# Batch 0's k and q loaded in layouts that TensorE turns, its first products in two halves, the residual summed apart, and a new order of the work

## The chip, the cores and the metric

The kernel runs on one core of a Trainium2 chip. The core has five engines that work side by side, each through its own list of instructions in order: TensorE (PE, the matrix products; PEld is its weight load), VectorE (DVE), ScalarE (ACT), GpSimd (POOL) and SyncE (SP), which issues the transfers from and to the chip's memory. The metric is the device time in microseconds (us); lower is better.

## The reference

Eight batches of 576 rows. For each batch there is first an attention without scores: q gets a softmax over the 64 channels of a head, k a softmax over the 576 rows, and the product of k and v (64x64 a head) is applied to q. The result x (576x512) goes through a gated feed-forward layer whose gate mixes rows.

```python
q_s = softmax(q, axis=-1)                  # over the 64 channels of a head
k_s = softmax(k, axis=2)                   # over the 576 rows
x = q_s @ (k_s.T @ v)                      # per head, 8 heads of 64 -> 576 x 512
u, v = gelu(x @ w_in) halves               # 512 each
v_n = (v - mean) / sqrt(var + 1e-6) * g_ln # over the 512 channels
v_s = w_sg @ v_n + b_sg                    # mixes the 576 rows
out = x + (u * v_s) @ w_out
```

## The kernel before

Everything is float32. The three large products (x with w_in, v_n with w_sg, the gated values with w_out) are made of three TensorE products each: both sides are split into a high part and a low part in a rounded type, and high by high, high by low and low by high are summed in one PSUM bank. The names end in `_h` and `_l` for these parts.

The work is cut into steps named after what they do, with the batch as first number, and one written list, `PLAN`, gives the order of all 1248 steps. The loop over `PLAN` calls the steps one after the other; the wrapper `InOrder` chains each engine's instructions, so every engine does its own part of the list in that order, and an engine whose next instruction waits holds back all that stands behind it. SP's transfers follow the list too. All of the recording goes through a few helper lines, so nearly all rows of the trace have one of two line numbers (L153 for the helper, L241 for TensorE).

The steps that matter here, for batch b and half h (four heads):
- Start: `load_w_in f` brings one of eight column blocks of w_in, 512 KB, as pairs of words; `wi_a` (ACT), `wi_b`, `wi_c`, `wi_d` (DVE) put float32 words together, `wi_h` (ACT) rounds the high part, and the low part is `wi_l`: either on another engine, or `wi_x` (TensorE: the word minus its high part, into PSUM) and a copy by ACT. Blocks 0 to 3 serve `hu`, blocks 4 to 7 `hv`. `w_sg` (`ws_`) and `w_out` (`wo_`) go the same way.
- k: `load_k`, the maximum over rows `k_ma`, `k_mb`, `k_mc` (DVE), then across partitions: for batches 0 and 1 by TensorE (`kt_mm`, `k_top`, `kb_mm`), for the others on DVE and ACT; `k_sub`, `k_exp`, the product with v `kv_mm`, `kv_inv`, `kv_scale`.
- q lies in 32-row blocks with half a head's channels in a row: `q_max`, `q_swapm`, `q_top`, `q_sub`, `q_exp`, `q_sum`, `q_swapd`, `q_inv`, `q_mul`, and `q_turn`, DVE's transpose in 32x32 blocks, which gives `qt` with channels on partitions.
- `x_mm` makes x, `x_high` and `x_low` split it (for batch 0 some low parts through `x_neg` on TensorE).
- `hu_mm` and `hv_mm` are x with w_in (four and, with the shared tail, four and a half a batch), `hu_gelu`, `hv_gelu` their activations, `hv_stat`, `hv_pow`, `hv_norm`, `hv_high`, `hv_low` the normalization and its split; `sg_mm` mixes rows, `gate`, `gate_high`, `gate_low` make the gated values, `out_mm` the last product, `out_add` adds x's high part out of PSUM, `out_rest` its low part, `out_store` stores. The very last block goes in two halves (`last_mm`, `last_add`, `last_rest`, `last_store`).

PSUM has three double banks (`ps2`, for x, hu, sg and out) and two single ones (`ps1`, for hv, kv and the small products), taken in turn; a product that takes a bank waits until the bank's reader is done. `kk`, `vv` and `qq` have two buffers each, one for each half.

## Time and profile before

| what | value |
|---|---|
| median of three runs | 515.95 us (515.62 to 517.37) |
| span of the profiled execution | 515.4 us |
| PE busy | 484.6 us (94%) |
| DVE busy | 365.9 us (71%) |
| ACT busy | 272.9 us (53%) |
| POOL busy | 125.3 us (24%) |

The span reaches from the first to the last instruction of the profiled execution; no other time of that execution is recorded, so what lies around the span is taken as the 0.55 us by which the median of the runs exceeds it. A busy share is an average over the whole span: in this kernel the stages have different limits, so the stretches are read one by one.

### The profile page before, as it was taken

How to read it: one execution, taken by the hardware profiler on the slowest of the kernel's cores; microseconds unless marked ns; L12 is line 12 of the kernel's file. 1: busy time of each engine (PE TensorE's matmuls, PEld its weight loads, DVE VectorE, ACT ScalarE, POOL GpSimd, SP SyncE). 2: the span in 40 equal slices, each digit the busy share in tenths (PEclk: the TensorE clock that was granted, in tenths of full speed). 3: DMA queues.
4: the chain of work that ended last, by engine and by line, in shares of the span. 5: the costliest groups of instructions: out<-in, count | busy, mean ns of one | idle time of the engine just before them, and what ended most of it. 6: DMA issues, size and time to landing. Idle time of an engine off the chain costs nothing.

```text
span 515.4 us, 9389 instructions
## 1 busy us (share of the span) xinstructions
PE 484.6 (94%) x3809; PEld 441.9 (86%) x3809; DVE 365.9 (71%) x640; ACT 272.9 (53%) x600; POOL 125.3 (24%) x106
## 2 busy tenths in 40 slices
PE   0678998999999999999999999999999999999996
PEld 0347876998999789998999889999989889999996
DVE  6999999999898998487956888658734662145222
ACT  4885977765763574755474356752439054323110
POOL 0333454333140430322023210112200311123312
PEclk9888999999999999999999999999999999999999
DMA  8977160031513402040421441033200020000103
GB/s 304 384 265 285 51 243 5 16 134 39 181 48 126 156 36 93 1 178 1 142 75 48 153 171 30 17 93 155 76 1 1 1 93 1 0 1 25 46 1 116
DMA packets 19055, 48.87 MB, mean 95 GB/s; under 512 B 1602, under 2 KB 8132, under 8 KB 19012
## 3 DMA queue, kind: packets, MB, share of 16 engines
q1 hardware_dynamic: 19012, 48.28, 26.5%
q8 instruction: 30, 0.49, 0.4%
q14 instruction: 13, 0.11, 0.1%
HBM read 38.83 MB, written 9.44 MB: 94 GB/s over the span
## 4 chain that ended last, share of the span: by engine, by line
PE 80%; DVE 12%; DMA 3%; issue 2%; ACT 1%; SPq 1%; POOL 0%; DVEq 0%; ACTq 0%
PE ps L241 80%; DVE km L153 2%; DMA kk<-k 2%; DVE ot_i L153 2%; DMA raw_vnh<-w_in 1%; DVE o L153 1%; DVE qm L153 1%; DVE v L153 1%; DVE qd L153 1%; DVE vnl L153 1%; DVE qt L153 1%; DVE qq L153 1%; DVE ulow L153 1%; DVE kk L153 1%; SPq L153 1%
## 5 line engine op out<-in xcount | busy, mean ns | idle before, releaser
L153 DVE TENSOR_TENSOR u<-ps,u 128x576 f32<-128x576 f32 x32 | 23.9, 751 | 60.7 <-PE ps L241 54.9
L241 PE MATMUL ps<-ulow,wo_h 128*128 128x288 f32 x256 | 55.5, 296 | 0.8 <-DVE ulow L153 0.8
L241 PE MATMUL ps<-ws_h,vnl 128*128 128x288 f32 x256 | 54.9, 295 | 0.8 <-DVE vnl L153 0.8
L241 PE MATMUL ps<-gh,wo_h 128*128 128x288 f32 x256 | 55.5, 295 | 0.0
L241 PE MATMUL ps<-gh,wo_l 128*128 128x288 f32 x256 | 55.4, 295 | 0.0
L153 POOL TENSOR_TENSOR rs<-ve,half 128x1 f32<-128x1 f32 x36 | 25.8, 723 | 118.8 <-DVE ve L153 118.8
L241 PE MATMUL ps<-ws_h,vnh 128*128 128x288 f32 x256 | 54.6, 294 | 0.0
L241 PE MATMUL ps<-ws_l,vnh 128*128 128x288 f32 x256 | 54.5, 293 | 0.0
L153 POOL TENSOR_TENSOR ulow<-u,gh 128x576 fp32r<-128x576 f32 x14 | 20.9, 1496 | 115.9 <-ACT gh L153 103.3
L153 ACT CAST gh<-u 128x576 fp32r<-128x576 f32 x32 | 21.3, 671 | 43.9 <-DVE u L153 43.8
L153 ACT ACTIVATE u<-ps 128x576 f32<-128x576 f32 x32 | 20.4, 649 | 44.7 <-PE ps L241 40.7
L241 PEld LDWEIGHTS ps<-ws_h,vnh 128*128 128x128 f32 x256 | 41.2, 188 | 2.0 <-issue 0.4
L241 PEld LDWEIGHTS ps<-gh,wo_h 128*128 128x128 f32 x256 | 41.5, 188 | 0.8
L241 PEld LDWEIGHTS ps<-ulow,wo_h 128*128 128x128 f32 x256 | 41.1, 188 | 1.1 <-DVE ulow L153 1.0
L241 PEld LDWEIGHTS ps<-ws_h,vnl 128*128 128x128 f32 x256 | 40.7, 187 | 1.0 <-DVE vnl L153 1.0
L241 PEld LDWEIGHTS ps<-gh,wo_l 128*128 128x128 f32 x256 | 41.4, 188 | 0.0
L241 PE MATMUL ps<-wi_h,x_h 128*128 128x512 f32 x144 | 40.3, 402 | 1.0 <-ACT v L153 1.0
L241 PE MATMUL ps<-x_h,wi_h 128*128 128x288 f32 x256 | 40.8, 302 | 0.5 <-DVE o L153 0.5
L153 ACT ACTIVATE v<-ps 128x512 f32<-128x512 f32 x36 | 21.5, 598 | 36.8 <-PE ps L241 27.2
L241 PEld LDWEIGHTS ps<-ws_l,vnh 128*128 128x128 f32 x256 | 41.0, 188 | 0.0
L241 PEld LDWEIGHTS ps<-x_h,wi_h 128*128 128x128 f32 x256 | 36.9, 192 | 3.2 <-DVE o L153 1.0
L241 PE MATMUL ps<-x_h,wi_l 128*128 128x288 f32 x256 | 39.6, 297 | 0.0
(116 smaller groups left out, 1085.7 us busy)
## 6 DMA issues: line engine op xcount, KB each, us to landing
vv<-v SPq DMA_DIRECT2D x16, 650.0 KB, 6.2
kk<-k SPq DMA_DIRECT2D x16, 640.0 KB, 4.2
qq<-q SPq DMA_DIRECT2D x16, 576.0 KB, 3.8
out<-o SPq DMA_DIRECT2D x31, 288.0 KB, 2.3
ghws<-w_sg SPq DMA_DIRECT2D x5, 320.0 KB, 8.7
raw_vnl<-w_in SPq DMA_DIRECT2D x2, 512.0 KB, 3.9
raw_vnh<-w_in SPq DMA_DIRECT2D x2, 512.0 KB, 7.3
raw_wo_l<-w_in SPq DMA_DIRECT2D x2, 512.0 KB
```

Source lines behind the costliest of these rows:

```text
L153: ins = op(*args, **kw)
L241: tc.keep_in_program_order(nc.tensor.matmul(*args, **kw))
```

## The change

The numbers of steps of most kinds stay the same. These parts are new:
- Batch 0's k is loaded with its channels on partitions and the rows along them (`k_turn`), into the buffer that later holds batch 0's `x_l`. Its maximum over rows is then one DVE reduction (`kr_max`), the exponential takes it as a bias on ACT (`kr_exp`), and TensorE turns the ten 128x128 blocks of a half (`ktr_mm`) into PSUM, from which ACT copies them to `kk` (`kr_copy`, `kr_rest`).
- Batch 0's q is loaded with rows on partitions and whole heads along them (`q_flat`): `qf_max`, `qf_sum` need no exchange between partitions (`qf_inv` is the reciprocal), the subtraction is on POOL, and TensorE turns five blocks for each pair of heads (`qtr_mm`), copied to `qt` by ACT (`qf_copy`).
- Batch 0's `hu` and `hv` come as `hu_first`, `hu_second`, `hv_first`, `hv_second`: the first takes the two channel blocks that come from x's first half, the second the other two, in the same bank.
- `out_base` adds x's two parts into the output buffer ahead of the product, on POOL (11 times) or DVE (21); `out_add` then adds the product. `out_rest` and `last_rest` are gone.
- Five memsets at the start go from DVE to POOL, `wi_a` of blocks 3 and 7 and one `wo_a` to POOL, some low parts and subtractions to other engines, and `PLAN` is a new list.

```diff
 PLAN = """
-load_w_in 3, wi_a 3, wi_b 3, wi_c 3, wi_d 3, load_w_in 2, load_w_in 1, load_b, load_w_in 0, load_q 0 1, load_eye, load_w_sg 3, load_q 0 0, load_k 0 0
+load_w_in 3, wi_a 3 G, wi_b 3, wi_c 3, load_k 0 0, kr_max 0 0, load_w_in 0, wi_a 0, wi_d 3, wi_h 3, load_eye, wi_b 0, load_q 0 1, wi_c 0, qf_max 0 1
...
-    V.memset(half, -0.5)
-    V.memset(f32(ws_2[TL:P]), 0.0)
-    V.memset(f32(vn_2[TL:P]), 0.0)
-    V.memset(f32(vn_2[TL:TL + 1]), 1.0)
-    V.memset(f32(vn_2[TL + 32:TL + 33]), 1.0)
+    G.memset(half, -0.5)
+    G.memset(f32(ws_2[TL:P]), 0.0)
+    G.memset(f32(vn_2[TL:P]), 0.0)
+    G.memset(f32(vn_2[TL:TL + 1]), 1.0)
+    G.memset(f32(vn_2[TL + 32:TL + 33]), 1.0)
...
-        def scale(f):
+        def scale(f, E=A):
 
             top, low, t = word(kind, f)
-            A.activation(f32(t), f32(top), AF.Copy, scale=2.0 ** -112)
+            if E is A:
+                A.activation(f32(t), f32(top), AF.Copy, scale=2.0 ** -112)
+            else:
+                E.tensor_scalar(out=f32(t), in0=f32(top), scalar1=2.0 ** -112, scalar2=None, op0=ALU.mult)
...
     def load_q(b, h):
-        Y.dma_start(out=qq_s(b, h, at=h), in_=q[b, h])
+        if b in FLAT:
+            Y.dma_start(out=qq_s(b, h, at=h), in_=q_flat[FLAT.index(b), h].rearrange("p t (g d) -> p t g d", d=D))
+        else:
+            Y.dma_start(out=qq_s(b, h, at=h, shape=[P, 2, 18, 32]), in_=q[b - sum(f < b for f in FLAT), h])
 
     def load_k(b, h):
-        Y.dma_start(out=kk_s(b, h, at=h), in_=k[b, h])
+        if b in TURN:
+            Y.dma_start(out=turned(b)[:, h], in_=k_turn[TURN.index(b), h])
+        else:
+            Y.dma_start(out=kk_s(b, h, at=h), in_=k[b - sum(t < b for t in TURN), h])
+
+    def turned(b):
+        return x_l("k", b, at=b, shape=[P, 2, 2, 5 * P], dt=F32)
+
+    def kr_max(b, h):
+        m = km_s(b, h, at=2 * b + h, shape=[P, 2])
+        V.tensor_reduce(out=m, in_=turned(b)[:, h, :, 0:S], axis=AX.X, op=ALU.max)
+        V.tensor_scalar(out=m, in0=m, scalar1=-1.0, scalar2=None, op0=ALU.mult)
+
+    def kr_exp(b, h):
+        t, m = turned(b)[:, h], km_s(b, h)
+        for a in range(2):
+            A.activation(t[:, a], t[:, a], AF.Exp, bias=m[:, a:a + 1])
+
+    def ktr_mm(b, h):
+        t = turned(b)[:, h]
+        wide, rest = bank(ps2, "kr", b, h), bank(ps1, "ks", b, h)
+        for i in range(5):
+            for a in range(2):
+                ps = rest[:, a * P:a * P + P] if i == ST else wide[:, i // 2, (i % 2) * 256 + a * P:(i % 2) * 256 + a * P + P]
+                mm(ps, t[:, a, i * P:i * P + P], eye, is_transpose=True, start=True, stop=True)
+
+    def kr_copy(b, h):
+        A.copy(out=kk_s(b, h, at=h)[:, 0:4].rearrange("p (j t) c -> p j (t c)", j=2), in_=st["kr", b, h])
+
+    def kr_rest(b, h):
+        A.copy(out=kk_s(b, h, at=h)[:, 4], in_=st["ks", b, h][:, 0:256])
+    def groups(b, h):
+        return qq_s(b, h, at=h).rearrange("p t g d -> p (t g) d")
+
+    def qf_max(b, h):
+        V.tensor_reduce(out=qm_s(b, h, at=h, shape=[P, 20]), in_=groups(b, h), axis=AX.X, op=ALU.max)
+
+    def qf_sub(b, h, E=G):
+        z = groups(b, h)
+        E.tensor_tensor(out=z, in0=z, in1=qm_s(b, h)[:, :, None].broadcast_to([P, 20, D]), op=ALU.subtract)
+
+    def qf_exp(b, h):
+        z = groups(b, h)
+        A.activation(z, z, AF.Exp)
...
+    def qf_mul(b, h, a, E=G):
+        z = qq_s(b, h)[:, :, 2 * a:2 * a + 2]
+        d = qd_s(b, h).rearrange("p (t g) -> p t g", g=4)[:, :, 2 * a:2 * a + 2, None].broadcast_to([P, 5, 2, D])
+        E.tensor_tensor(out=z, in0=z, in1=d, op=ALU.mult)
+
+    def qtr_mm(b, p):
+        z, ps = qq_s(b, p // 2), bank(ps2, "qt", b, p)
+        for i in range(5):
+            to = ps[:, i // ST, (i % ST) * P:(i % ST) * P + P]
+            mm(to, z[:, i, 2 * (p % 2):2 * (p % 2) + 2].rearrange("p g d -> p (g d)"), eye, is_transpose=True, start=True, stop=True)
+
+    def qf_copy(b, p):
+        A.copy(out=qt_s(b, p, at=p), in_=st["qt", b, p].rearrange("p j n -> p (j n)")[:, 0:S])
...
-    def three(ps, pairs, n):
+    def three(ps, pairs, n, first=True, last=True):
         for m, (l, r) in enumerate(pairs):
             for j in range(2):
-                mm(ps[:, j, 0:n], l, r[j], start=m == 0, stop=m == len(pairs) - 1)
+                mm(ps[:, j, 0:n], l, r[j], start=bool(first and m == 0), stop=bool(last and m == len(pairs) - 1))
...
+    def hv_some(b, i, cs, first, last):
+        col = ST * P if i == ST else (b % 2) * TL + i * P
+        if first:
+            for z in (v_s, mv_s, s6_s, ve_s, rs_s):
+                z.take(b, i)
+            bank(ps1, "hv", b, i)
+        ph, pairs = st["hv", b, i], [(l, r, c) for l, r in ((x_h, wi_h), (x_l, wi_h), (x_h, wi_l)) for c in cs]
+        for m, (lhs, rhs, c) in enumerate(pairs):
+            mm(ph, lhs(b)[:, c, col:col + P], rhs[:, c, DV:2 * DV], start=first and m == 0, stop=last and m == len(pairs) - 1)
...
+    def hu_some(b, f, h):
+        fs, cs = slice(f * P, (f + 1) * P), (2 * h, 2 * h + 1)
+        pairs = [(w[:, c, fs], halves(x(b)[:, c])) for w, x in ((wi_h, x_h), (wi_l, x_h), (wi_h, x_l)) for c in cs]
+        three(st["u", b, f] if h else bank(ps2, "u", b, f), pairs, HS, not h, h)
...
+    def out_base(b, e, E=G):
+        E.tensor_tensor(out=o_s(b, e, at=4 * b + e), in0=f32(x_h(b)[:, e, 0:S]), in1=f32(x_l(b)[:, e, 0:S]), op=ALU.add)
+
     def out_add(b, e):
-        V.tensor_tensor(out=split(o_s(b, e, at=4 * b + e)), in0=st["o", b, e][:, :, 0:HS], in1=f32(split(x_h(b)[:, e, 0:S])), op=ALU.add)
-
-    def out_rest(b, e, E=G):
-        o = o_s(b, e)
-        E.tensor_tensor(out=o, in0=o, in1=f32(x_l(b)[:, e, 0:S]), op=ALU.add)
+        o = split(o_s(b, e))
+        V.tensor_tensor(out=o, in0=st["o", b, e][:, :, 0:HS], in1=o, op=ALU.add)
...
     def last_add(b, j):
-        o, xh, xl, js = last(b, j)
-        V.tensor_tensor(out=o, in0=st["o", b, 3][:, j, 0:HS], in1=xh, op=ALU.add)
-
-    def last_rest(b, j, E=V):
-        o, xh, xl, js = last(b, j)
-        E.tensor_tensor(out=o, in0=o, in1=xl, op=ALU.add)
+        o = o_s(b, 3)[:, j * HS:j * HS + HS]
+        V.tensor_tensor(out=o, in0=st["o", b, 3][:, j, 0:HS], in1=o, op=ALU.add)
...
+    qf = qo[FLAT].transpose(0, 2, 1, 3).reshape(-1, S, 2, 256)
+    qf = np.concatenate([qf, qf[:, ST * P:]], axis=1)
+    arr["q_flat"] = np.ascontiguousarray(qf.reshape(-1, 5, P, 2, 256).transpose(0, 3, 2, 1, 4))
...
+    arr["k_turn"] = np.ascontiguousarray(ks[TURN].reshape(-1, 5 * P, 2, 2, P).transpose(0, 2, 4, 3, 1))
```

`PLAN` alone is 104 lines; how it moves instructions is seen engine by engine. TensorE's rows ahead of the first product of q with k and v (`qt`, `kvt`), first before, then of the change. `eye` is the identity, `km` and `kt` the maxima of k, `x_lk` the turned k, `ghws` the raw w_sg, `ot_i` a word block of w_in.

```order
L241 MATMUL ps_1_80<-eye,kt_1_235 128x128 x2
L241 MATMUL ps_0_79<-vv_0_128,kk_0_112 64x65 x20
L241 MATMUL ps_1_80<-vv_1_139,kk_1_122 64x65 x20
L241 MATMUL ps_0_79<-ot_i_195,eye 128x512
L241 MATMUL ps_0_79<-wi_h,minus 128x512
L241 MATMUL ps_2_78<-qt_0_310,kvt_0_308 64x288
```

```order
L243 MATMUL ps_2_77<-eye,x_lk_98 128x128 x8
L243 MATMUL ps_1_79<-eye,x_lk_98 128x128 x2
L243 MATMUL ps_0_78<-vv_0_175,kk_0_150 64x65 x20
L243 MATMUL ps_1_79<-vv_1_204,kk_1_171 64x65 x20
L243 MATMUL ps_0_75<-eye,qq_0_134 128x128 x5
L243 MATMUL ps_1_76<-eye,qq_0_134 128x128 x5
L243 MATMUL ps_2_77<-eye,qq_1_110 128x128 x5
L243 MATMUL ps_0_75<-qt_0_240,kvt_0_263 64x288
```

The small products for k's maxima are gone for batch 0, and blocks of k and q are turned on TensorE where `qt` came from DVE.

DVE's first rows, before and of the change (`qm`, `qd` are q's maxima and sums; `raw_` are words of w_in):

```order
L153 MEMSET half 128x1
L153 MEMSET ws_66 64x640
L153 MEMSET vn_73 64x512
L153 MEMSET vn_73 1x512 x2
L153 TENSOR_SCALAR ot_i_95<-ot_i_95 128x512
L153 SCALAR_TENSOR_TENSOR ot_i_95<-raw_vnl,ot_i_95 128x512 x2
L153 TENSOR_SCALAR ot_i_115<-ot_i_115 128x512
L153 SCALAR_TENSOR_TENSOR ot_i_115<-raw_vnl,ot_i_115 128x512
L153 TENSOR_SCALAR ot_i_118<-ot_i_118 128x512
```

```order
L156 TENSOR_SCALAR ot_i_94<-ot_i_94 128x512
L156 SCALAR_TENSOR_TENSOR ot_i_94<-raw_vnl,ot_i_94 128x512
L156 TENSOR_REDUCE km_0_100<-x_lk_98 128x2
L156 TENSOR_SCALAR km_0_100<-km_0_100 128x2
L156 SCALAR_TENSOR_TENSOR ot_i_94<-raw_vnl,ot_i_94 128x512
L156 TENSOR_SCALAR ot_i_104<-ot_i_104 128x512
L156 SCALAR_TENSOR_TENSOR ot_i_104<-raw_vnh,ot_i_104 128x512
L156 TENSOR_REDUCE qm_1_113<-qq_1_110 128x20
L156 SCALAR_TENSOR_TENSOR ot_i_104<-raw_vnh,ot_i_104 128x512
L156 TENSOR_REDUCE qm_0_143<-qq_0_134 128x20
L156 TENSOR_REDUCE km_1_147<-x_lk_98 128x2
```

Before, DVE's list opens with memsets and four blocks of w_in; in the change it opens with one block, k's and q's maxima come between the parts of the second, and the other blocks stand behind.

ACT's rows around the first gate of batch 0 (`gh` its high parts), before and of the change; a table load stands ahead of the first exponential (`kk`, `qq`) after a gelu (`u`, `v`) and the other way round. Over the whole list there are 22 of them before and 34 in the change.

```order
L153 ACT_TABLE_LOAD
L153 ACTIVATE v_0_1127,sm_0_1128<-ps_0_79 128x512
L153 CAST gh_2_1133<-u_2_608 128x576
L153 CAST vn_73<-vn_72 64x512
L153 CAST gh_3_1179<-u_3_898 128x576
L153 ACTIVATE u_0_1208<-ps_0_76 128x576
```

```order
L156 ACT_TABLE_LOAD
L156 ACTIVATE v_3_1132<-ps_0_78 128x512
L156 COPY qe_1_1141<-qd_1_1127 32x36 x4
L156 COPY ka_1_1225<-kf_1_1092 32x8 x4
L156 COPY kb_1_1267<-kf_1_1092 32x8 x4
L156 ACTIVATE vnh<-v_3_1132,rs_3_1255 128x512
L156 ACTIVATE u_2_1316<-ps_0_75 128x576
L156 ACT_TABLE_LOAD
L156 ACTIVATE kk_1_832<-kk_1_832 128x1280
L156 ACTIVATE vnh<-v_1_938,rs_1_947 128x512
L156 ACT_TABLE_LOAD
L156 ACTIVATE u_0_1372<-ps_2_77 128x576
```

In the change a single exponential of k stands between two gelus here, with a load on either side of it.

## Rows read from the trace of the kernel before

**Rows 1.** Stretches: length; busy PE, PEld, DVE, ACT, POOL (count); clock, DMA share, GB/s.

```profile
0.00:13.00 13.00, 0.59 (x1) 0.50 (x2) 8.28 (x16) 5.96 (x10) 0.20 (x4) 1.00 0.86 306
13.00:43.86 30.86, 21.03 (x157) 12.01 (x156) 30.69 (x52) 25.23 (x50) 12.05 (x9) 0.88 0.94 333
43.86:87.54 43.68, 42.64 (x310) 35.92 (x309) 41.25 (x74) 32.18 (x77) 18.22 (x15) 0.97 0.35 127
87.54:90.29 2.75, 2.01 (x15) 1.77 (x13) 2.63 (x8) 2.49 (x8) 0.55 (x1) 1.00 0.00 0
...
130.00:400.00 270.00, 270.00 (x2145) 250.71 (x2144) 200.73 (x357) 151.16 (x335) 53.87 (x45) 1.00 0.24 84
...
500.00:515.40 15.40, 10.86 (x81) 10.55 (x80) 5.22 (x9) 0.00 (x0) 2.85 (x2) 0.97 0.26 97
```

**Rows 2.** TensorE's timeline: start us, length us, instruction, [idle before, releaser].

```profile
34.01 1.12 PE L241 MATMUL ps<-ot_i,eye 128*128 128x512 f32 x2
...
35.30 1.20 PE L241 MATMUL ps<-qt,kvt 64*64 64x288 f32 x16
...
43.18 1.03 PE L241 MATMUL ps<-eye,km 128*128 128x128 f32 x4 [1.91 <-DVE km L153]
43.86 2.27 PE L241 MATMUL ps<-x_h,wi_h 128*128 128x288 f32 x8
...
87.54 0.42 PE L241 MATMUL ps<-ws_h,vnh 128*128 128x288 f32 x2
...
90.34 0.54 PE L241 MATMUL ps<-ws_h,vnl 128*128 128x288 f32 x2 [0.79 <-DVE vnl L153]
```

**Rows 3.** ACT's timeline: the first block of w_in, and the fourth.

```profile
4.21 0.66 ACT L153 ACTIVATE ot_i<-raw_vnl 128x512 f32<-128x512 f32 x1 [2.20 <-DMA raw_vnl<-w_in]
...
10.59 0.67 ACT L153 ACTIVATE ot_i<-raw_vnh 128x512 f32<-128x512 f32 x1 [0.18 <-DMA raw_vnh<-w_in]
```

**Rows 4.** Groups by form: count, busy us, mean ns of one, idle before.

```profile
L153 DVE STREAM_TRANSPOSE qt<-qq 128x576 f32<-128x576 f32 x32 | 24.4, 766 | 6.8 <-PE ps L241 4.9 <-POOL qq L153 2.0
...
L153 DVE TENSOR_REDUCE qm<-qq 128x36 f32<-128x1152 f32 x16 | 21.4, 1338 | 0.0
...
L153 DVE TENSOR_TENSOR qq<-qq,qd 128x576 f32<-128x576 f32 x13 | 12.0, 943 | 0.1
L153 DVE TENSOR_TENSOR km<-kk 128x512 f32<-128x512 f32 x16 | 11.7, 734 | 0.6 <-DMA kk<-k 0.6
...
L153 DVE TENSOR_TENSOR qq<-qq,qm 128x1152 f32<-128x1152 f32 x7 | 10.1, 1440 | 0.0
L153 DVE TENSOR_TENSOR km<-km 128x256 f32<-128x256 f32 x16 | 9.4, 599 | 0.1
...
L153 DVE TENSOR_TENSOR kk<-kk,ps 128x1280 f32<-128x1280 f32 x4 | 5.9, 1482 | 1.2 <-PE ps L241 1.2
...
L153 POOL TENSOR_TENSOR qq<-qq,qm 128x1152 f32<-128x1152 f32 x9 | 19.3, 2149 | 38.6 <-DVE qm L153 25.6 <-issue 13.0
...
L153 ACT ACTIVATE kk<-kk 128x1280 f32<-128x1280 f32 x16 | 20.3, 1271 | 6.0 <-DVE kk L153 5.8
```

**Rows 5.** Timelines of POOL and DVE while both work on SBUF.

```profile
15.10 2.13 POOL L153 TENSOR_TENSOR qq<-qq,qm 128x1152 f32<-128x1152 f32 x1 [14.66 <-DVE qm L153]
...
16.21 1.56 DVE L153 TENSOR_TENSOR km<-kk 128x512 f32<-128x512 f32 x1
```

**Rows 6.** ACT's timeline around its first switch from exponential to gelu.

```profile
57.66 1.28 ACT L153 ACT_TABLE_LOAD   x1
58.95 1.20 ACT L153 ACTIVATE u<-ps 128x576 f32<-128x576 f32 x2
```

**Rows 7.** What TensorE waited for: us in total, times, longest.

```profile
PE ps L241 <- ACT v L153: 1.0, 1, 1.0
```

**Rows 8.** DVE's last instructions, the first and the last of four.

```profile
510.89 0.46 DVE L153 TENSOR_TENSOR o<-ps,x_h 128x288 f32<-128x288 f32 x1 [2.44 <-PE ps L241]
...
512.25 0.46 DVE L153 TENSOR_TENSOR o<-o,x_l 128x288 f32<-128x288 f32 x1
```

More of the change, by code (lines that the diff above doesn't have):

```diff
@@ new lines @@
+x_low 0 1 A, k_ma 1 0, ws_x 3, wi_c 1, wi_a 6, k_mb 1 1, ws_l 3 A, kv_scale 0 1, x_mm 0 1, load_b, wi_d 1, wi_h 1, load_q 1 0, x_high 0 2, wi_b 6
+load_q 1 1, k_mc 1 1, wi_c 6, wi_x 1, wi_l 1 A, k_mb 1 0, wi_d 7, x_neg 0 2, hu_first 0 0, wi_l 2 A, x_low 0 2 A, q_max 1 0, q_swapm 1 0, wi_h 7
+wi_d 6, kt_mm 1 1, hu_first 0 2, x_high 0 3, k_mc 1 0, kt_mm 1 0, k_top 1 1, q_top 1 0, load_w_in 4, q_sub 1 0 G, q_max 1 1, kb_mm 1 1, k_top 1 0
+x_low 0 3, hu_second 0 2, k_sub 1 1 V, hu_second 0 0, wi_a 4, wi_h 6, wi_l 7 G, b_h, load_w_in 5, wi_a 5, q_exp 1 0, hu_first 0 1, wi_b 5, wi_b 4
@@ L182, in gmlp_kernel @@
 @with_exitstack
-def gmlp_kernel(ctx: ExitStack, tc: tile.TileContext, q, k, v, w_in, g_ln, w_sg, b_sg, w_out, identity, blocks, out):
+def gmlp_kernel(ctx: ExitStack, tc: tile.TileContext, q, q_flat, k, k_turn, v, w_in, g_ln, w_sg, b_sg, w_out, identity, out):
     nc = tc.nc
@@ new lines, in qf_exp, with qf_sum, qf_inv @@
+    def qf_exp(b, h):
+        z = groups(b, h)
+        A.activation(z, z, AF.Exp)
+    def qf_sum(b, h):
+        V.tensor_reduce(out=qd_s(b, h, at=h, shape=[P, 20]), in_=groups(b, h), axis=AX.X, op=ALU.add)
+    def qf_inv(b, h):
+        d = qd_s(b, h)
+        V.tensor_scalar(out=d, in0=d, scalar1=1e-9, scalar2=None, op0=ALU.add)
+        V.reciprocal(out=d, in_=d)
+    def qf_mul(b, h, a, E=G):
+        z = qq_s(b, h)[:, :, 2 * a:2 * a + 2]
+        d = qd_s(b, h).rearrange("p (t g) -> p t g", g=4)[:, :, 2 * a:2 * a + 2, None].broadcast_to([P, 5, 2, D])
+        E.tensor_tensor(out=z, in0=z, in1=d, op=ALU.mult)
@@ L392, in k_mc @@
-    def k_mc(b, h):
+        E.tensor_tensor(out=m[:, 0:256], in0=m[:, 0:256], in1=m[:, 256:512], op=ALU.max)
+    def k_mc(b, h, E=V):
         m = km_s(b, h)
-        V.tensor_tensor(out=m[:, 0:256], in0=m[:, 0:256], in1=kk_s(b, h)[:, 4], op=ALU.max)
+        E.tensor_tensor(out=m[:, 0:256], in0=m[:, 0:256], in1=kk_s(b, h)[:, 4], op=ALU.max)
     def columns(ps):
@@ L489, in q_mul @@
     def q_mul(b, h, a, E=G):
[L490 removed]
+        q3 = qq_s(b, h)[:, a]
         E.tensor_tensor(out=q3, in0=q3, in1=qd_s(b, h, at=h)[:, a * 18:a * 18 + 18, None].broadcast_to([P, 18, 32]), op=ALU.mult)
[L493 to L523 removed]
     def q_turn(b, p):
[L526 removed]
+        V.transpose(out=qt_s(b, p, at=p), in_=qq_s(b, p // 2)[:, p % 2].rearrange("p j c -> p (j c)"))
     def sums(ps):
@@ L593, in x_low, with hv_first, hv_second @@
                 V.tensor_tensor(out=to, in0=ps, in1=f32(hi), op=ALU.subtract)
-    def hv_mm(b, i):
-        col = ST * P if i == ST else (b % 2) * TL + i * P
-        for z in (v_s, mv_s, s6_s, ve_s, rs_s):
-            z.take(b, i)
-        ph, m = bank(ps1, "hv", b, i), 0
-        for lhs, rhs in ((x_h, wi_h), (x_l, wi_h), (x_h, wi_l)):
-            for c in range(4):
-                mm(ph, lhs(b)[:, c, col:col + P], rhs[:, c, DV:2 * DV], start=m == 0, stop=m == 11)
-                m += 1
+    def hv_some(b, i, cs, first, last):
[7 more added lines that the diff above has]
+            mm(ph, lhs(b)[:, c, col:col + P], rhs[:, c, DV:2 * DV], start=first and m == 0, stop=last and m == len(pairs) - 1)
+    def hv_mm(b, i):
+        hv_some(b, i, range(4), True, True)
+    def hv_first(b, i):
+        hv_some(b, i, (0, 1), True, False)
+    def hv_second(b, i):
+        hv_some(b, i, (2, 3), False, True)
     def hv_gelu(b, i, E=V):
```

268 lines of the change are left out of this document (120 added, 148 removed).

## The prediction

> **What bounds the kernel now.** I read the busy share by stretches first, because the shares of the whole span mix stages. TensorE never stops between 130 and 400 us, and the 10.86 us of the last 15.40 are its final products and the way out [rows 1]. A change that leaves the number of products alone can gain only where TensorE stands still: 12.41 us in the first 13, 9.83 in the next 30.86, 1.04 up to the first gate product at 87.54, 0.74 right behind it, and 4.54 at the end [rows 1]. Nearly all of that is the start.
>
> What ends the waits there? The first block of w_in can be used at 4.21 us and the fourth at 10.59 [rows 3]: loads come first. From 13.00 to 43.86 DVE works 30.69 of 30.86 us, and 41.25 of 43.68 in the next stretch, while ACT and POOL have room [rows 1]. So after the loads DVE sets the pace, to just behind 90 us: there TensorE still waits 0.79 us for DVE's last `vnl` of batch 0 [rows 2]. Three marks carry my sum: the first product that makes x (35.30), the first of x with w_in (43.86) and the first gate product (87.54) [rows 2]. Behind the third mark the steps of TensorE that are left are the same in kind and number before and after, so what is won there stays won unless new waits arise.
>
> **The first mark.** In the new list the loads stand as w_in block, k, w_in block, identity, q, w_sg, q, k (the other half), two w_in blocks, v, v. Between the first and the fourth w_in block 1.57 MB landed in 6.38 us [rows 3]; later the queue moves 333 GB/s at a share of 0.94, so about 0.36 MB/us when full [rows 1]. By that, as estimates: k's first half at 6.9 us, q's first at 11.5, q's second at 14.2, k's second at 16.0, v at 20.8 and 22.6.
>
> From there I place the steps one behind the other. A reduction of 1280 values is 1.338 x 1280/1152 = 1.49 us, POOL's subtraction 2.149 x 1280/1152 = 2.39, an exponential 1.27, a multiplication of 640 values 0.943 x 640/576 = 1.05 [rows 4]. q's first maximum ends at 13.0, POOL's subtraction at 15.4; the second maximum at 15.7, its subtraction at 18.1. k's second maximum ends at 17.4 on DVE, and ACT does three exponentials in a row: 16.7, 18.8, 20.1. DVE then has sum, reciprocal (0.5, estimate) and one multiplication of the first half (17.5 to 20.6), the second half's sum, reciprocal and two multiplications: 24.7. Five blocks are turned on TensorE and copied by ACT, which no row shows. Four turns of 128x128 stand in 0.68 us [rows 2], so five take 0.85; a copy of 576 columns should be near 0.65 us; not less than half of either, and not more than twice. The first product of x comes at 26.2, against 35.30: 9.1 us earlier. POOL's `wi_a` of the first block and POOL's memsets have no row; they delay DVE's first step to between 4.9 and 6.5, but DVE then waits for q at 11.5 anyway, and that covers them.
>
> **The second mark.** DVE frees k's and v's product at 25.7 and has twelve instructions up to the second half's; the mean of one in the start is 30.69/52 = 0.59 [rows 1], so 7.1 at most (three are very short): 6.5, to 32.2. Then x's second half, one `wi_x` (34.01 to 35.30: 1.29 [rows 2]) and one small product: 3.0. The first of `hu_first` starts at 35.2, 8.7 earlier than 43.86. Its split in two halves lets it start on x's first half; alone it costs nothing, since the products are the same, and it is covered as long as the second half of x comes within two half products.
>
> **The third mark.** The stretch from the second to the third mark takes 43.68 us, 1.04 of it waiting [rows 1]. The new one holds the same steps of TensorE, plus one `wi_x` (1.29) and four small turns (0.68) that stood ahead of it before [rows 2]: 44.6. I add 1.0 for two places where only half a product covers a split of x. 35.2 + 45.6 = 80.8.
>
> DVE has to agree. It had 8.28 + 30.69 + 41.25 + 2.63 = 82.85 us of work up to 90.29 [rows 1]. Ahead of the same `vnl` the new list has two `kk` subtractions less (2.96), two of q (2.88), four turns (3.06), eight steps of k's maximum (two of 0.734, three of 0.599, three near 0.4: 4.5), one q maximum that now comes later (1.34); it has two reductions of k more (2.7), three multiplications (3.1), longer reductions (0.6) and a few low parts (0.7): 7.6 us less, and the memsets leave too. With the same 7.4 us of idle time, and up to 2 more while it waits for q, that `vnl` ends 6 to 8 us earlier, and the gate product may start at 79.5 to 81.5. Both ways meet; I take 80.8, which is 6.7 us earlier.
>
> **Behind it.** The residual's sum costs the same number of passes as before; only at the very end does it shorten the chain. There four DVE steps follow TensorE, 510.89 to 512.71, and two remain: 0.9 us less [rows 8]. The base sums ahead of them have the last products as cover; uncovered, one would cost 1.6 on POOL at the rate of its 1152-wide passes halved and rounded up (1.1 to 2.1) [rows 4].
>
> **Sum.** 515.4 - 6.7 - 0.9 = 507.8 us of span, and 0.55 around it: 508.3. With the parts' bounds (first mark from 25 to 28.5, second from 33.4 to 37.5, 0 to 2.5 of waits, DVE's 2 us) the likeliest case lies between 505 and 511.
>
> **The rivals.**
>
> DVE is held up by POOL. Where POOL ran a subtraction from 15.10, a DVE step of k that takes 0.734 on average took 1.56 [rows 4, 5]: 0.83 lost. In the new start POOL subtracts both halves of q and multiplies a quarter, that last while DVE multiplies its own quarter, so DVE may lose about 1.2 us there and 0.83 at three or four other steps: some 4 us ahead of the third mark, 512.3. The Trainium skill (GPSIMD Engine Reference, Key points) says that GpSimd shares its SBUF interfaces with VectorE and collides with DVE instructions that read two SBUF inputs or run in a two-port mode. The long row agrees. By that rule reductions are spared.
>
> Against it: two of DVE's three long steps while POOL subtracts are reductions, and the reductions' mean of 1.338 over all 16 leaves no room for long ones [rows 4].
>
> Table loads. The new list has 34 of ACT's table loads against 22. One takes 1.28 us, and the next gelu starts 1.29 after it [rows 6]: 15.4 us more for ACT, which has room. They cost time only where TensorE has nothing else: before, TensorE waited for an activation `v` once, for 1.0 us [rows 7]. If the new order left all twelve bare, 508.3 + 15.4 = 523.7; it is slower than before from eight bare loads on (9.2 us above my forecast). Against it: all the switches of the kernel before left that one wait. The Trainium skill (ScalarE: Activation LUTs, What ACT_TABLE_LOAD costs) counts a switch at 2.66 us, with a drain behind the load. By that twelve would be 32 us of ACT, and four bare ones would suffice; the row shows no drain behind the load, so I stay with 1.28.
>
> The middle breaks. Before, not a tenth of a microsecond is lost from 130 to 400 [rows 1]. A new order can only lose there: six waits of 0.8, the size of the one in rows 2, would make 513. For it speaks that POOL now has subtractions of k (2.4 each) and base sums between short steps that others wait for; against it that DVE's work ahead of each mark is smaller, so its results lie further ahead.
>
> The gain is taken back by w_in. The new list puts blocks 1, 2 and 4 to 7 behind q and k, and SP's load of the next k waits for the product of batch 0's k and v (about 22 us), with blocks 6, 4 and 5 queued behind it. About 4.3 MB later, near 37 us by the rate above, the last lands; `hv` needs it near 48. That cover of about 10 us less its conversion must be gone before anything is lost; if it is, the time comes back to 513 to 516, no change.
>
> **How the numbers follow.** The case above 0.50, DVE held up by POOL 0.16, the middle 0.13, w_in 0.10, table loads 0.07, and 0.04 for a better start than placed (503). About 0.3% (1.5 us) is what a measurement here can tell from no change, so 514.4 to 517.5 is "same". Faster: 0.50 + 0.16 + 0.12 + 0.02 + 0.04 = 0.84; same 0.08; slower 0.08. The range reaches from 504.5 to 514.5: it leaves out the table loads, most of the w_in case and the best start.
>
> **What would show it.** In the new trace: x's first product at 25 to 28.5, `hu_first` at 33.4 to 37.5, the first gate product at 79 to 83, no stretch from 130 to 400 with more than 1 us of idle TensorE, two DVE steps behind the last product. DVE's two-input steps beside POOL at more than 1.2 us speak for the first rival, waits of TensorE for `u` or `v` right behind table loads for the second. Wrong I am if the marks hold but the time doesn't (the middle), or if the first mark holds and the third doesn't.

## The result, and the profile after

The changed kernel takes 511.12 us (median of 4 runs, 510.1 to 512.72) against 516.46 for the kernel before (median of 4, 515.62 to 517.37). The ratio is 0.9903, with a 95% interval of 0.9877 to 0.9929: faster by 5.3 us, where 7.65 was forecast.

The profiled execution is the one of 510.1 us, with a span of 508.3. In every run whose span is known, 1.7 to 2.1 us lie around it, so the 0.55 us that the prediction added was too little by about 1.3. So the profiled execution of before (span 515.4) was one of about 517.3, near the top of its runs; the two traces lie 7.1 us apart, the medians 5.3.

Stretches of the changed kernel, columns as in [rows 1]; the third begins at the second mark's old place and ends at the new third mark:

```profile
0.00:13.00 13.00, 3.69 (x10) 2.46 (x11) 6.85 (x10) 5.65 (x9) 5.13 (x11) 1.00 0.87 328
13.00:43.86 30.86, 27.84 (x247) 22.03 (x246) 29.55 (x51) 26.89 (x48) 11.51 (x7) 1.00 0.97 338
43.86:77.30 33.44, 33.00 (x245) 25.79 (x244) 31.52 (x63) 28.05 (x65) 15.17 (x14) 1.00 0.46 157
...
130.00:400.00 270.00, 266.79 (x2091) 245.54 (x2090) 194.30 (x343) 160.81 (x344) 71.62 (x53) 1.00 0.22 76
500.00:508.30 8.30, 4.05 (x30) 3.72 (x28) 2.13 (x4) 0.00 (x0) 0.00 (x0) 0.86 0.30 110
```

TensorE's timeline, the three marks and its waits (compare [rows 2]):

```profile
9.31 2.07 PE L243 MATMUL ps<-ot_i,eye 128*128 128x512 f32 x2 [9.31 <-DVE ot_i L156]
...
25.03 1.45 PE L243 MATMUL ps<-qt,kvt 64*64 64x288 f32 x16
...
31.18 1.20 PE L243 MATMUL ps<-qt,kvt 64*64 64x288 f32 x16 [0.74 <-DVE kvt L156]
...
33.76 0.69 PE L243 MATMUL ps<-x_h,wi_h 128*128 128x288 f32 x4
...
77.30 0.43 PE L243 MATMUL ps<-ws_h,vnh 128*128 128x288 f32 x2
...
137.26 1.85 PE L243 MATMUL ps<-qt,kvt 64*64 64x288 f32 x16 [0.52 <-DVE u L156]
...
217.34 0.54 PE L243 MATMUL ps<-ulow,wo_h 128*128 128x288 f32 x2 [0.95 <-POOL ulow L156]
...
231.07 1.39 PE L243 MATMUL ps<-vv,kk 128*64 128x65 f32 x40 [1.23 <-ACT kk L156]
```

The marks stand at 25.03, 33.76 and 77.30 us, against 35.30, 43.86 and 87.54 [rows 2]. From 13.00 us to the third mark TensorE is idle for 3.46 us, and the granted clock is 1.00 where it was 0.88 and 0.97. So the start gives 10.24 us. Behind the third mark 3.4 come back: from the first gate product to the start of the last product it was 423.03 us (510.57 less 87.54), and is now 426.45. From 130 to 400 us TensorE now stands still for 3.21 us; before for none. From the end of the last product to the end of the span it is 4.26 us, before 4.54. Together: -10.24 + 3.42 - 0.28 = -7.1.

Timelines of DVE and POOL while POOL subtracts q, the two steps of DVE that x's second half waits for, and DVE's last two sums (compare [rows 5, 8]):

```profile
8.49 0.17 DVE L156 TENSOR_SCALAR km<-km 128x2 f32<-128x2 f32 x1
...
13.62 1.34 DVE L156 TENSOR_REDUCE km<-x_lk 128x2 f32<-128x1152 f32 x1
15.00 1.82 DVE L156 TENSOR_SCALAR km<-km 128x2 f32<-128x2 f32 x1
...
28.58 1.29 DVE L156 TENSOR_TENSOR km<-kk 128x512 f32<-128x512 f32 x2 [0.86 <-DMA kk<-k]
...
30.73 0.30 DVE L156 TENSOR_TENSOR kvt<-ps,kr 128x128 f32<-128x128 f32 x1
...
504.15 0.82 DVE L156 TENSOR_TENSOR o<-ps,o 128x288 f32<-128x288 f32 x2 [2.60 <-PE ps L243]
...
11.80 5.00 POOL L156 TENSOR_TENSOR qq<-qq,qm 128x1280 f32<-128x1280 f32 x2 [5.79 <-DVE qm L156]
```

Groups of the operations that had no row before (columns as in [rows 4]):

```profile
L243 PE MATMUL ps<-eye,x_lk 128*128 128x128 f32 x20 | 3.9, 352 | 1.4 <-ACT x_lk L156 1.4
L243 PE MATMUL ps<-eye,qq 128*128 128x128 f32 x20 | 2.8, 278 | 0.5 <-DVE qq L156 0.5
...
L156 ACT ACT_TABLE_LOAD x34 | 43.6, 1283 | 10.3 <-issue 4.3 <-DVE vnl L156 2.6 <-DVE kf L156 2.3
L156 ACT COPY qt<-ps 128x576 f32<-128x576 f32 x4 | 2.6, 646 | 0.9 <-PE ps L243 0.9
L156 ACT COPY kk<-ps 128x1024 f32<-128x1024 f32 x2 | 2.0, 1017 | 0.4 <-PE ps L243 0.4
```

A copy to `qt` takes 0.646 us (0.65 was forecast), and the 34 table loads took 43.6 us of ACT without a single wait of TensorE for ACT's `u` or `v`.

One load stands in the chain of the changed kernel's start. The second half of x needs `kvt` of its half (`kv_scale 0 1`), and in DVE's queue this step stands behind the first maxima of batch 1's k (`km<-kk`), which wait for the load of that k. The load's two halves are issued at 21.56 and 22.74 us, as the product of batch 0's k and v (20.08 to 22.66) frees their buffers. In the six traces that share this part of the list (the changed kernel and the five in the part on mending), `km<-kk` starts between 28.23 and 28.80 us, TensorE waits for that `kvt` each time (0.74 us at 31.18 here), and the first gate product comes 48.69 to 48.72 us behind `km<-kk`.

### The profile page after: what moved, and what is told of

Its sections match the earlier page's. It is cut to its first block, busy times and chain, and to the rows that moved or that the text cites. A ratio compares the mean times of both kernels' runs of the same rounds, so it can differ in the third digit from the quotient of the medians.

```text
span 508.3 us, 9454 instructions
## 1 busy us (share of the span) xinstructions
PE 487.6 (96%) x3841; PEld 445.5 (88%) x3841; DVE 351.9 (69%) x622; ACT 287.5 (57%) x603; POOL 140.7 (28%) x114
## 5 line engine op out<-in xcount | busy, mean ns | idle before, releaser
L156 ACT ACT_TABLE_LOAD x34 | 43.6, 1283 | 10.3 <-issue 4.3
L156 POOL TENSOR_TENSOR ulow<-u,gh 128x576 fp32r<-128x576 f32 x16 | 23.5, 1468 | 83.0 <-ACT gh L156 76.0
L243 PE MATMUL ps<-wi_h,x_l 128*128 128x512 f32 x144 | 40.7, 397 | 0.4 <-DVE x_l L156 0.4
L243 PE MATMUL ps<-wi_l,x_h 128*128 128x512 f32 x144 | 40.1, 394 | 0.0
L243 PE MATMUL ps<-x_l,wi_h 128*128 128x288 f32 x256 | 40.0, 296 | 0.0
```

The source lines that it names most:

```text
L156: ins = op(*args, **kw)
L243: tc.keep_in_program_order(nc.tensor.matmul(*args, **kw))
```

## The experiments

All ratios are to runs of the kernel before on the same chip. Edits of the list are shown as its steps, not as its long lines.

### The parts undone in the new list

**k_undone.** Batch 0's k as before:

```diff
-kr_max 0 0
+k_ma 0 0, k_mb 0 0, k_mc 0 0
...
-kr_exp 0 0, wi_x 3, ktr_mm 0 0
+kt_mm 0 0, wi_x 3, k_top 0 0, kb_mm 0 0, k_sub 0 0 V, k_exp 0 0
...
-kr_copy 0 0, kr_rest 0 0
```

> The changed kernel, with batch 0's k alone back in its old layout and steps (maxima on DVE, two small turns and a broadcast on TensorE for each half, the subtraction on DVE), at the places of the new list. Theory A (what DVE no longer does sets the start): DVE gets 0.73 + 0.60 + about 0.4 + 0.2 + 1.48 us for each half in place of one reduction of about 1.5, so 1.9 more for each, 3 to 4 in all; x's first product comes 3 to 5 us later than 25.0, the first gate product 3 to 4 later than 77.3, the time is 514 to 515.5. Theory B (the order of the loads and steps is what gained): marks within 1 us, 511 to 512.5.

517.28 us, ratio 1.0018 (0.9999 to 1.0037). In this kernel and in order_alone the low part of w_in's block 0 is read from a bank that k's broadcast has already overwritten, so their results are not the reference's; the work on each engine is what the edit says. The marks: 32.40, 40.71, 84.24. The third comes 6.9 us later, twice what theory A priced. The stretch and TensorE's waits show that DVE is not fuller than in the changed kernel, but emptier (27.27 us against 29.55):

```profile
13.00:43.86 30.86, 23.33 (x189) 16.80 (x189) 27.27 (x45) 19.91 (x34) 7.81 (x5) 0.83 0.83 285
...
16.69 0.64 PE L243 MATMUL ps<-ws_h,minus 128*128 128x320 f32 x1 [2.90 <-ACT ws_h L156]
26.21 1.92 PE L243 MATMUL ps<-vv,kk 128*64 128x65 f32 x40 [3.20 <-ACT wi_l L156]
```

**q_undone.** Batch 0's q as before:

```diff
-qf_max 0 1
+q_max 0 1, q_swapm 0 1, q_top 0 1
...
-qf_sum 0 1, qf_inv 0 1
+q_sum 0 1, q_swapd 0 1, q_inv 0 1
...
-qtr_mm 0 0, qf_copy 0 0
+q_turn 0 0
```

> The changed kernel, with batch 0's q alone back in its old layout and steps (exchanges of 32 partitions on ACT for maximum and sum, the four turns to qt on DVE), at the places of the new list. Theory A: DVE gets four turns of 0.77 us, 3.1 in all, and TensorE loses twenty small turns of 0.28; the first gate product 2 to 4 us later than 77.3, the time 513 to 515. Theory B: marks within 1 us, 511 to 512.5.

523.89 us, ratio 1.0152 (1.0121 to 1.0183): slower than the kernel before. The marks: 33.45, 44.06, 87.59. Theory A gave the direction, but 2 to 4 us at the third mark, where 10.3 were measured. DVE's work in 13 to 43.86 us is only 22.07 us; it waits for the exchanges, which stand in ACT's queue, and TensorE waits for DVE:

```profile
24.52 0.20 DVE L156 SCALAR_TENSOR_TENSOR qd<-qd,qe 128x36 f32<-128x36 f32 x1 [4.00 <-ACT qe L156]
...
33.45 2.20 PE L243 MATMUL ps<-qt,kvt 64*64 64x288 f32 x16 [8.46 <-DVE kvt L156]
```

**halves_undone.** hu and hv of batch 0 whole:

```diff
-hu_first 0 2
...
-hu_second 0 2
+hu_mm 0 2
...
-hv_first 0 3, hv_second 0 3
+hv_mm 0 3
```

> The changed kernel, with hu and hv of batch 0 as whole products at the places of their second halves. If the halves only let TensorE begin earlier and DVE sets the pace up to the first gate product: the second mark (first product of x with w_in) 1 to 4 us later, the third within 1 us of 77.3, 511 to 512. If TensorE's early start is what counts: the third mark and the time 2 to 4 us later, 513 to 515.

516.49 us, ratio 1.0 (0.9977 to 1.0022). The marks: 25.42, 36.92, 83.33. That is the second case, TensorE's early start counts, at more than its price: 6.0 us at the third mark where 2 to 4 were expected. Of the 6.0, 3.2 are there at the second mark; behind it TensorE waits more, and from 66.2 to 69.5 us its granted clock is 0.50 (1.2 GHz), right behind the last two waits below. They stand at places that half products fill in the changed kernel:

```profile
35.13 0.44 PE L243 MATMUL ps<-eye,km 128*128 128x128 f32 x2 [0.90 <-ACT wi_l L156]
36.40 0.44 PE L243 MATMUL ps<-eye,km 128*128 128x128 f32 x2 [0.83 <-DVE km L156]
...
64.82 0.67 PE L243 MATMUL ps<-qt,kvt 64*64 64x288 f32 x2 [1.55 <-DVE qt L156]
66.19 2.19 PE L243 MATMUL ps<-qt,kvt 64*64 64x288 f32 x14 [0.70 <-DVE qt L156]
```

**order_alone.** All three undone at once (the edits above together).

> The changed kernel with k, q and the halves of batch 0 all undone: what is left of the change is the new list's order, the base sums of the residual and the steps that changed engines. Theory A: the start's gain is gone, the first gate product at 84 to 88, the time 516 to 520 (what the single undoings cost, added up, and the middle's loss of about 3 us on top of it). Theory B: the third mark stays below 81 and the time below 514.

532.58 us, ratio 1.0324 (1.0283 to 1.0365); third mark 101.43, granted clock 0.74 from 13 to 43.86 us. The new order without the parts costs 16 us. Theory B, as I wrote it, is out, and theory A's numbers (84 to 88, 516 to 520) are far too low. The single undoings cost 6.9, 10.3 and 6.0 us at the third mark, 23.3 in all, close to the 24.1 that all three cost together, and more than twice what the whole change wins there: the list was made for these parts, so an undoing prices the part and its misfit together. The price holds the clock, too: from 13 to 43.86 us the granted clock is 0.83 in k_undone and q_undone and 0.74 here, where the changed kernel has 1.00.

### The parts alone in the old list

**k_turned_in_old_list.**

```diff
-k_ma 0 0, k_mb 0 0, k_mc 0 0
+kr_max 0 0, kr_exp 0 0
...
-kt_mm 0 0, k_top 0 0, kb_mm 0 0, k_sub 0 0, k_exp 0 0
+ktr_mm 0 0, kr_copy 0 0, kr_rest 0 0
```

> The kernel before, with one part of the change alone: batch 0's k loaded with channels on partitions, its maximum one reduction, ten blocks of each half turned on TensorE. Everything else, the list's order too, is the old one. DVE loses about 1.9 us of work for each half. Theory A (what DVE no longer does sets the start, whatever the order): the first gate product 2.5 to 4 us earlier than 87.5, the time 512.5 to 514. Theory B (a part pays only with the order that was made for it): the marks within 1 us, the time 515.5 to 517.

519.68 us, ratio 1.008 (1.0058 to 1.0103): slower. DVE's work in 13 to 43.86 us falls from 30.69 [rows 1] to 24.34 us, and x's first product still comes at 36.38, the gate product at 88.48. Theory A fails here: DVE was full, was relieved of 6.35 us, and nothing came earlier. Waits of TensorE, ACT and DVE in a row:

```profile
24.64 0.33 PE L242 MATMUL ps<-eye,x_lk 128*128 128x128 f32 x1 [3.75 <-ACT x_lk L154]
...
23.75 1.55 ACT L154 ACTIVATE x_lk<-x_lk,km 128x640 f32<-128x640 f32 x2 [1.51 <-DVE km L154]
...
29.61 0.20 DVE L154 SCALAR_TENSOR_TENSOR qd<-qd,qe 128x36 f32<-128x36 f32 x1 [4.04 <-ACT qe L154]
```

In the old order k's second half is reduced late, its exponential waits for that, the exchange of q's sums stands behind it on ACT, and DVE waits 4.04 us for the exchange. What DVE saved, it spends waiting.

**one_half_in_old_list.**

```diff
 x_neg 0 2
+hu_first 0 2
...
-hu_mm 0 2
+hu_second 0 2
```

> The kernel before, with one product of hu (batch 0, block 2) in two halves, the first of them ahead of the small turns of batch 1's k, at which TensorE waits 1.91 us in the old trace. If TensorE's idle time between x's halves is what the halves win, as undoing them in the changed kernel suggests: the first product of x with w_in 2 to 2.6 us earlier than 43.86, the first gate product 1 to 2 earlier than 87.5, the time 1 to 2 less than before. If DVE sets the pace up to the gate, as the prediction says of the kernel before: second mark earlier, third mark and time within 0.5.

515.56 us, ratio 0.9995 (0.998 to 1.0009): no change. Second mark 39.97, third 85.28. TensorE's first product came 1.16 us earlier in this execution (11.25 against 12.41 [rows 1]; across the traces of the old list it lies between 11.04 and 12.60), so 2.7 and 1.1 us are left for the edit. One half product fills most of the wait for `km` (0.35 us are left of it), and part of the gain goes into the next wait, 1.43 us for `x_l` at 45.61. In this execution the clock also stays at 1.00 behind the second mark, where before it fell to 0.50. The trace leans to the first case, the times to the second; the size isn't settled.

**base_in_old_list.** All 32 sums, here those of batch 7:

```diff
+out_base 7 2 V
 out_mm 7 2
...
-out_rest 7 2 V
...
-last_rest 7 0
...
-last_rest 7 1
```

> The kernel before, with the residual's two parts summed ahead of each product, on the engine that added the second part before, everything else in the old order. By the prediction only the end gains, two DVE steps less: 0.9 us from the end of TensorE's last product to the end, 4.54 to about 3.6, the time 515.0 to 515.6. By the trace of the changed kernel, where the two last stores leave together and land later: 4.2 to 4.4, the time within 0.3 of before. It also shows a second time how long TensorE takes from the first gate product to its last product in the old order (423.0 in the one trace, 426.5 to 427.8 in the new list): within 1 us of 423.0 if the new order costs those microseconds, 425 or more if they vary from run to run.

519.37 us, ratio 1.0079 (1.0048 to 1.011): slower. The end does take 0.8 less (3.76 us). But from the gate to the last product TensorE now takes 426.90 us, where the other two kernels in the old order take 423.24 and 423.01, as before 423.03. So these microseconds belong to the list: the old order varies by 0.23 us over three traces. The waits, and what makes the first of them:

```profile
113.61 0.54 PE L241 MATMUL ps<-ulow,wo_h 128*128 128x288 f32 x2 [2.01 <-DVE ulow L153]
...
287.20 0.53 PE L241 MATMUL ps<-gh,wo_h 128*128 128x288 f32 x2 [1.63 <-DVE o L153]
...
111.61 1.95 DVE L153 TENSOR_TENSOR ulow<-u,gh 128x576 fp32r<-128x576 f32 x1
...
111.41 1.53 POOL L153 TENSOR_TENSOR o<-x_h,x_l 128x576 f32<-128x576 f32 x1
```

The base sum on POOL began 0.2 us ahead of DVE's low part, which then took 1.95 us in place of 0.75 and came too late. A base sum is no dearer than the old second sum, but it stands in front of work that TensorE waits for, where the old one stood behind.

### Mending the changed kernel

**last_add_early.**

```diff
-last_mm 7 0, last_mm 7 1, out_store 7 0, last_add 7 0, last_store 7 0
+last_mm 7 0, last_add 7 0, last_store 7 0, last_mm 7 1, out_store 7 0
```

> The changed kernel with the sum and the store of the last output block's first half ahead of its second half's products, in place of behind them. In the trace both sums start at 504.15, right behind the very last product, and the two stores land 2.4 us after issue, against 1.8 before. If the first sum waits for the last product only because no earlier product signals: it starts near 502.5, the last store goes out about 0.4 us earlier and has the queue to itself; from the end of the last product to the end of the span 3.2 to 3.6 us in place of 4.26, the time 0.6 to 1.0 less, 510.1 to 510.5. If the stores' landing doesn't depend on each other: 0.4 less. If the products of the second half then wait for the first sum (same tile): no change or up to 1 us more.

510.57 us, ratio 0.9908 (0.9873 to 0.9943): no change against 0.9903 that these times can tell. The trace shows both named effects: the sum starts at 502.92 and the end takes 3.22 us, but the second half's products wait for it.

```profile
503.43 0.40 PE L243 MATMUL ps<-gh,wo_h 128*128 128x288 f32 x1 [0.61 <-DVE o L156]
```

**negate_on_act.**

```diff
     def kr_max(b, h):
...
-        V.tensor_scalar(out=m, in0=m, scalar1=-1.0, scalar2=None, op0=ALU.mult)
...
     def kr_exp(b, h):
...
+        A.mul(m, m, -1.0)
```

> The changed kernel with the negation of k's maxima (two elements for each partition) on ACT, just ahead of the exponential, in place of DVE. There one of the two took 1.82 us beside POOL's subtraction of q, the other 0.17. If DVE really stood still there and sets the pace up to x's first product: that product 0.7 to 1.0 us earlier than 25.0, the first gate product about as much earlier than 77.3, the time 0.5 to 1.0 less, 510.1 to 510.6. Rival: whatever two-byte-wise short DVE instruction stands next to POOL's subtraction takes the long time in its place, and the marks stay within 0.3. Second rival: the stall has no share in the marks, since TensorE is busy with other blocks: x's product earlier, the gate product not.

510.4 us, ratio 0.9882 (0.9858 to 0.9907): not told apart from 0.9903. The long step is gone and no other takes its place, but DVE then waits 0.88 us for the exponential of q, and the marks stay (25.50, 77.47). That looks like the second rival, but the run doesn't settle it. In this execution TensorE ran at half clock for a while, of which the changed kernel's trace shows nothing. In it the products of batch 0's k and v took 4.13 us in place of 2.58, so the load of batch 1's k, which waits for them, went out late, and DVE waited for it longer than before:

```profile
20.00:22.00 2.00, 2.00 (x42) 2.00 (x40) 1.90 (x5) 2.00 (x4) 0.06 (x1) 0.50 0.73 239
...
28.78 1.29 DVE L156 TENSOR_TENSOR km<-kk 128x512 f32<-128x512 f32 x2 [1.64 <-DMA kk<-k]
```

**first_block_on_act.**

```diff
-wi_a 3 G, wi_b 3, wi_c 3, load_k 0 0, kr_max 0 0
+wi_a 3, wi_b 3, wi_c 3, wi_d 3, load_k 0 0, kr_max 0 0
```

> The changed kernel with the first scaling of w_in's first block (wi_a 3) on ACT, which stands idle until 7.47 us, in place of POOL, and with that block's last step on DVE (wi_d 3) ahead of k's first maximum. POOL took 1.52 us for it, ACT takes 0.66, so DVE can begin at about 5.1 in place of 6.04. If DVE is the engine that everything waits for from there: TensorE's first product 0.6 to 1.0 us earlier than 9.31, x's first product 0.5 to 0.9 earlier, the time 510.2 to 510.7. Rival, the loads: k's first half lands just at 7.1, q's first just ahead of 10.2, so what DVE gains it then spends waiting for DMA; x's product within 0.2 us, no change in time.

511.44 us, ratio 0.9911 (0.9881 to 0.994): no change. TensorE's first product comes at 8.38, x's at 24.36, the gate product at 76.93: of 0.93 us 0.37 are left at the third mark. TensorE now waits for the identity and DVE for q, so the loads take over. What decides at the later marks is again the load of batch 1's k: its maximum starts 0.35 us earlier than in the changed kernel (28.23 against 28.58), and so do the second and the third mark, by 0.37 us:

```profile
8.38 2.05 PE L243 MATMUL ps<-ot_i,eye 128*128 128x512 f32 x2 [8.38 <-DMA eye<-identity]
...
12.26 1.49 DVE L156 TENSOR_REDUCE qm<-qq 128x20 f32<-128x1280 f32 x1 [0.32 <-DMA qq<-q_flat]
...
28.23 1.29 DVE L156 TENSOR_TENSOR km<-kk 128x512 f32<-128x512 f32 x2 [1.03 <-DMA kk<-k]
```

**middle_mended.**

```diff
-k_maxb 4 1, q_turn 4 2, out_store 1 2, k_maxa 4 0, sg_mm 2 3, gate 2 3, gate_low 2 1 V
+out_store 1 2, sg_mm 2 3, gate 2 3, gate_low 2 1 V, k_maxb 4 1, q_turn 4 2, k_maxa 4 0
...
+k_sub 4 0 V
 q_sum 5 0
...
-k_sub 4 0 G
```

> The changed kernel with two places of the middle reordered: batch 2's last gate (and one low part) on DVE ahead of the exchange steps of batch 4's k maximum, and batch 4's first subtraction of k on DVE, ahead of the sum of q, in place of POOL. In the trace TensorE waits 0.25 and 0.95 us there for low parts of the gate (215.24, 217.34) and 1.23 for batch 4's exponential (231.07). If these waits are a loss of their own: they go, the stretch from 200 to 300 us has less than 0.5 us of idle TensorE in place of 2.51, and the time falls by 2.0 to 2.4, to about 509. Rival (the time is given back by the next mark that is late, since DVE only does other work first): idle time in the stretch above 1.5 us, the time within 0.7.

509.14 us, ratio 0.9866 (0.9845 to 0.9888), 1.9 us under the changed kernel by the ratios (0.37% of 516; the intervals just overlap). The three waits are gone or under 0.1 us, and one of 0.65 for `kvt` is new; the stretch now idles for 0.93 us, nearer to the first case than to the rival:

```profile
200.00:300.00 100.00, 99.07 (x833) 91.65 (x832) 75.71 (x137) 61.86 (x130) 31.57 (x24) 1.00 0.23 80
```

From the gate to the last product it takes 424.85 us; the four traces of the new list with all its parts and the old middle lie between 426.45 and 427.83 (427.49 of last_add_early holds its 0.61 us wait).

**four_mended.** The four edits above together.

> The changed kernel with the four edits tried singly, all together: the last sum ahead of the last products, the negation of k's maxima on ACT, the first block's scaling on ACT, and the middle's two places reordered. If they add up: 0.6 at the end, 0.5 at the start (two edits in the same chain), 2.0 in the middle, so about 508.0 to 508.6, and the span behind the first gate product below 425.5. If the start's edits only let TensorE begin earlier and wait later: 508.3 to 509.2.

508.55 us, ratio 0.9867 (0.983 to 0.9905): no better than the middle alone. Its 426.58 us behind the gate hold two waits that the trace of middle_mended lacks: the 0.61 us of last_add_early, which the shorter end gives back, and one of 1.06 us. The load of batch 7's k took 1.0 us longer to land (9.1 against 8.1), and DVE's queue passes that on:

```profile
358.89 0.69 DVE L156 TENSOR_TENSOR km<-kk 128x512 f32<-128x512 f32 x1 [1.66 <-DMA kk<-k]
...
363.50 1.20 PE L243 MATMUL ps<-qt,kvt 64*64 64x288 f32 x16 [1.06 <-DVE kvt L156]
```

So 508.6 to 509.1 us is the fastest that was found. Both kernels are faster than the one before; that they beat the changed kernel rests on two ratios that lie 0.4% below its own, with intervals that overlap.

## Why the prediction came out as it did

**The sum.** 511.12 us lies inside the stated range and just above the likeliest case's 505 to 511, but partly by luck. The forecast of the span, 7.6 us less, met 7.1 because errors cancel: 3.5 us too little at the third mark, 3.4 us given back behind it that the sum put at nothing, and 0.6 too much at the tail. The 2.8 us between 508.3 and 511.12 are 0.5 of this, 1.2 for what lies around the span (1.8 us and not 0.55), and 1.0 by which the median lies above the profiled execution. Two of the prediction's own signs failed: the gate product came ahead of 79 to 83, and TensorE stands still for more than 1 us from 130 to 400. By its last sentence (the first mark holds and the third doesn't) the account was wrong, on the good side.

**The first mark**: 25.03, forecast 26.2. The turns and copies cost what was bounded. The loads landed earlier than estimated: q's first maximum began at 10.23 us, not at 11.5. Wrong was the sentence that DVE waits for q at 11.5 anyway: from 6.04 us on DVE works nearly without a stop, so POOL's first `wi_a` (4.49 to 6.01) does delay it; the memsets, over at 3.1, do not. In first_block_on_act this is worth 0.9 us at the first product and 0.4 at the gate; in four_mended, with the same edit, the identity lands later, the first product comes at 9.23 and the gate product at 77.28, and nothing is left of it.

**The second mark**: 33.76, forecast 35.2, all but 0.3 of the difference from the first. But the path was another: between the two `kvt` I counted DVE's work alone, 6.5 us. It took 6.3, of which 0.86 are the wait for the load of batch 1's k, which the prediction named only under the w_in rival and not here.

**The third mark**: 77.30, forecast 80.8, the step that was most off. From the second to the third it took 43.54 us, forecast 45.6. The 1.0 us for splits covered by half a product came to less: TensorE waited 0.44 us in the whole stretch, 0.36 of it for one `x_l`. And the 44.6 us of products took 43.10, since the clock stood at 1.00, where the rows that I summed had 0.97. Before, the start of this stretch, behind a wait of 1.91 us [rows 2], ran at half clock:

```profile
43.86:46.80 2.94, 2.94 (x14) 2.94 (x13) 2.94 (x6) 2.60 (x7) 1.30 (x1) 0.50 1.06 406
```

Half of these 2.94 us is 1.5, just what the products took less; so part of what the change wins ahead of the gate is the clock, which in the changed kernel's trace doesn't fall there. That the halves cost nothing was right; that they only let TensorE begin early was too low a price, as halves_undone shows (6.0 us at the third mark).

**What set the pace.** "After the loads DVE sets the pace" was half right for the kernel before, and misled about the cure. DVE was full there, but k_turned_in_old_list takes 6.35 us of work from it and gains nothing, and q_undone has DVE at 22.07 of 30.86 us and is slower than the kernel before. As the waits in these traces read, the start is bound by a chain that passes between ACT, DVE and TensorE, each of which takes its work in order; the new layouts shorten the chain (no exchange of q's maxima and sums over ACT, no broadcast of k's maximum over TensorE), and the new order has each link in its queue when its input comes. In the changed kernel the load of batch 1's k is a link of it; with `km<-kk` behind `kv_scale 0 1` in DVE's queue x's second half would not wait for that load; this is worth at most the 0.74 us at 31.18, and no run tried it. Nor was q alone tried in the old list. My sum of DVE's work was too small: up to the end of batch 0's last `vnl` DVE works 68.84 us, 14.0 less than the 82.86 before, where 7.6 and the memsets (2.1) were forecast; that step ends at 78.21, 12.1 us earlier and not 6 to 8. Among what I left out are the steps of q's maxima behind the exchange (1.6 us), w_out's low parts (1.4) and a step of batch 2's k (1.3).

**Behind it**: "what is won there stays won unless new waits arise" was true, and they arose: 3.4 us are given back. This is the rival of the middle, at 3.4 in place of the 4.7 us between 508.3 and 513, together with a better start than forecast. New waits of 0.25 us and more come to 3.41 us, and old ones of 2.96 are gone (one of them in rows 2), so in net they account for 0.45, and shorter waits for 0.3. In the other 2.7 us TensorE is busy: the same 3344 products take longer, some at the change from one kind to the next, the others by a nanosecond or two each, and what makes this stays open. Of the new waits, middle_mended takes away 2.43: they came from one gate queued behind exchange steps and from one subtraction of k on POOL. The wait of 0.52 us at 137.26 is the first rival at another place (below). "The residual's sum costs the same number of passes as before" was the wrong way to cost it: base_in_old_list shows that the place counts, and that base sums alone cost 3.9 us there. How much of the new list's loss is theirs was not tried.

**The tail**: forecast 0.9, measured 0.28. Two sums fewer did save 0.8 in base_in_old_list. In the changed kernel's trace the two last stores were issued 0.43 us apart and took 2.3 us to land (median), before 0.86 apart and 1.7. But k_undone's, 0.42 us apart, took 1.8, so the distance alone doesn't explain it. Across the nine traces with two sums and the old order of the last steps the end takes 3.76 to 5.21 us, so the term is right and smaller than that scatter.

**The rivals.** Table loads: refuted, 34 loads and no wait of TensorE for ACT's `u` or `v`. w_in: no wait for it at `hv`, refuted. DVE held by POOL: it happens, as below, and at 15.00 us it costs DVE 1.65 us. In negate_on_act the marks don't move when that is taken away, but the half clock and the late load in that execution hide what it is worth; it stays open.

## What to carry to other kernels

When an engine is full in the stretch that matters, ask whether the next instruction in the chain waits for its work or for its turn: taking work away helps only where the queues of the other engines hold the next link at that moment. A step that is moved from behind a product to ahead of it costs the same time and delays everything queued behind it; look who waits there. The same goes for a step that waits for a load: in an in-order queue all that stands behind it waits for that load, too. And price a part both ways, undone in the new order and alone in the old: where these don't agree, part and order belong together.
